# A Mamba-2 scan and a low-rank mixer on one core: a new order for the first third of a hand-kept instruction list, and a last tile in two halves

## The chip, the cores and the metric

One of the eight cores of a Trainium2 chip. The metric is device time in microseconds for one execution, the median of several runs. Engines: PE (TensorE, matmuls; PEld is its weight load), DVE (VectorE), ACT (ScalarE), POOL (GpSimd), SP (SyncE, which issues DMAs here).

## The reference

```
# scan: x (4,8,768,32), a (4,8,768), B and C (4,8,768,16)
cum = cumsum(log(clip(a)))                    # in chunks of 32 positions
M   = (C B^T) * exp(cum_i - cum_j) * causal   # within a chunk
y   = M x + (C state) * exp(cum)
state = exp(sum) * state + sum_j B_j x_j exp(cum_last - cum_j)
# bridge: y -> x2 (4, 768, 256): batch, position, channel
# mixer: U (768,32), V (32,768), w_ch1 (256,1024), w_ch2 (1024,256)
u   = x2 + ((x2^T U) V)^T
out = u + relu(u w_ch1) w_ch2
```

The scan's inputs and the output are float32. U, V, w_ch1 and w_ch2 arrive as 64-bit floats, and the kernel first makes them into 32-bit numbers from their words.

## The kernel before

**Tiling.** The scan works on twelve pairs of blocks of 128 positions (three pairs for each of four batches; eight heads together). The mixer of a batch works on two halves of 384 positions and eight blocks of 128 of the 1024 hidden columns.

**Order.** Nothing is scheduled by a tool: PLAN (line 34) is a list of words, and follow (line 915) goes through it and issues each word's instructions. Every engine runs its own in that order, so a word's place decides what stands behind what on each queue. The words, with pair k, batch b, half j, hidden block m:

- Loads, all issued on SP: Bk (two loads of B, one of C), Xk (two loads of x), U, V (four loads), w0 to w8 (pieces of the two weights). A leading Y marks the early ones. B, X and w without Y are held (line 920, `until`) until the last DVE instruction issued before that word is done, and SP stands still meanwhile.
- c1 to c9: one step each of making a weight piece into 32 bits (to_fp32, line 409): first two DVE word steps and one ACT step, then one DVE word step, then one POOL addition; c0 converts U, C0 converts V. v spreads V over the partitions (spread, line 872): an ACT rounding into Vn, a DVE subtraction in UV (line 875), sixteen small matmuls (line 880), four ACT copies.
- A0, A1: the decays (line 369). K: the factors between chunks.
- Scan of a pair: P or Q (multiply B and C by decays, DVE, line 466), T or V (transposes on PE, then ACT and DVE copies T and Cm), g (sixteen matmuls, line 522), m and M (DVE masks, four in all), s (sixteen matmuls, line 556), u (DVE updates of S, then Sm on POOL, line 583), i and j (line 646, j waiting for a small DVE copy into `settled` or for another DVE instruction of that turn), n (32 matmuls, line 681), y (two ACT copies out of PSUM, line 693), t or O (transposes back, line 701).
- Mixer of batch 0: p, q (lines 728 and 746), a (line 756 and a DVE addition to yT), U b.j.m (first weight, plain float32, two matmuls over 384 positions, line 800), d (second weight, output, line 831). Batches 1 to 3 use f, e, h in place of U, with weights split by R and activations split by S.
- Fn: the next PSUM tile that is asked for is first written by n blocks of a 128-column product with the identity (fill and idle, lines 132 and 156). A second F ahead of the next tile replaces the first.

The words tiles hold the 64-bit words; there are 15 of them. PSUM has eight tiles, two for each of the tags w, x, z and y.

**The last tile.** d3.1.0.5 is the list's last word. When an output tile (128 positions, 256 channels) has its last product, lines 854 to 856 add it on DVE to ytok and store it from SP.

Of the kernel before, what the change touches and what calls it, by code (L numbers as in the profile page):

```python
# [23 lines left out]
ALU = mybir.AluOpType  # L24
# [7 lines left out]


PLAN = (
    'F3 YU0 c0 A0 YB0 Q0.1 Q0.0 A1 F2 Q0.2 V0.0.0 YX0 YB1 V0.1.1 c0 Q1.0 YX1 F1 K0 s0 g0 Q1.2 m0 '
    'V1.0.2 YB2 Q1.1 V1.1.2 M0 n0 YX2 u0 g1 i0 s1 Q2.0 M1 YV0 j0 y0 m1 Q2.2 Q2.1 V2.0.2 F1 u1 '
    'V2.1.3 C0 C0 n1 C0 YB3 w1 i1 g2 j1 y1 w0 m2 B5 s2 F3 X3 c0 M2 v0 B4 O0.0 u2 t1 i2 n2 j2 P3 T3 '
    'c1 y2 T3 O2.1 c2 p0 P5 g3 w4 T5 m3 M3 q0 c1 c1 w2 c2 T5 n3 a0.1 X4 a0.0 s3 U0.1.0 c2 U0.1.1 B6 '
    'P4 T4 u3 w3 w6 T4 U0.0.1 c5 c5 i3 c3 c5 g4 j3 y3 s4 w5 m4 U0.0.0 U0.1.6 c3 U0.1.7 M4 c3 X5 u4 '
    'U0.0.6 B8 c4 U0.0.3 P6 t3 c4 T6 T6 i4 R0 g5 R3 n4 s5 c7 M5 U0.0.7 c4 U0.1.5 U0.0.4 w8 j4 y4 w7 '  # L40
    'X6 c7 c7 m5 B9 U0.1.3 c6 U0.0.2 c6 c6 U0.1.4 u5 n5 i5 B7 g6 c9 j5 y5 M6 c9 t4 c9 U0.0.5 U0.1.2 '
    'd0.0.1.0 m6 c8 c8 B10 R1 t5 d0.0.2.0 R5 d0.0.2.1 p1 c8 d0.0.2.2 X7 q1 R6 d0.0.1.1 P7 d0.0.1.2 '
    'R0 T7 R2 R1 T7 a1.0 d0.0.2.3 d0.0.1.3 a1.1 d0.1.0.0 S1.0 P10 d0.1.0.1 d0.1.0.2 d0.1.0.3 s6 R3 '
    'R2 X8 g7 n6 m7 X9 P9 M7 X11 f1.0.0 u6 f1.0.4 f1.0.1 e1.0.0 h1.0.0 f1.0.5 e1.0.4 h1.0.4 e1.0.1 '
    'f1.0.6 i6 s7 d0.0.0.0 R5 R4 f1.0.7 h1.0.1 R4 d0.0.0.1 P8 u7 T8 T8 e1.0.6 h1.0.6 e1.0.7 '
    'd0.0.0.2 d0.0.0.3 h1.0.7 e1.0.5 f1.0.2 h1.0.5 j6 f1.0.3 d0.1.2.0 e1.0.2 y6 e1.0.3 R6 d0.1.1.0 '
    'h1.0.2 X10 S1.1 d0.1.1.1 T9 T9 d0.1.1.2 h1.0.3 d0.1.1.3 d0.1.2.1 d0.1.2.2 d0.1.2.3 s8 n7 i7 u8 '
    'g8 R7 j7 m8 M8 s9 R7 f1.1.0 R7 R4 R5 d1.0.0.0 d1.0.0.1 d1.0.0.2 d1.0.0.3 u9 e1.1.0 d1.0.1.0 '
    'f1.1.7 d1.0.1.1 d1.0.1.2 h1.1.0 y7 f1.1.6 R6 e1.1.7 d1.0.0.4 d1.0.0.5 t7 d1.0.1.3 e1.1.6 '
    'h1.1.6 d1.0.2.0 d1.0.2.1 d1.0.2.2 h1.1.7 f1.1.4 d1.0.2.3 d1.0.1.4 d1.0.1.5 f1.1.1 d1.0.2.4 B11 '  # L50
    'e1.1.4 h1.1.4 e1.1.1 d1.0.2.5 h1.1.1 t6 f1.1.3 f1.1.2 f1.1.5 e1.1.3 e1.1.2 h1.1.2 i8 n8 s10 j8 '
    'e1.1.5 d1.1.0.0 d1.1.2.0 d1.1.2.1 d1.1.1.0 P11 d1.1.1.1 u10 h1.1.3 d1.1.1.2 d1.1.0.1 d1.1.2.2 '
    'd1.1.0.2 h1.1.5 d1.1.0.3 d1.1.1.3 y8 d1.1.2.3 d1.1.0.4 d1.1.1.4 d1.1.0.5 d1.1.2.4 d1.1.2.5 '
    'd1.1.1.5 t8 i9 g9 m9 T10 T10 M9 p2 n9 q2 g10 m10 M10 T11 T11 j9 a2.0 s11 g11 u11 y9 m11 i10 '
    'S2.0 M11 n10 t9 f2.0.0 f2.0.4 e2.0.0 f2.0.1 h2.0.0 f2.0.5 e2.0.1 h2.0.1 f2.0.2 j10 e2.0.4 y10 '
    'e2.0.5 e2.0.2 f2.0.3 h2.0.4 i11 n11 h2.0.5 h2.0.2 e2.0.3 f2.0.6 f2.0.7 h2.0.3 j11 y11 a2.1 '
    'e2.0.7 e2.0.6 h2.0.6 d2.0.0.0 S2.1 h2.0.7 t10 t11 d2.0.0.1 d2.0.0.2 f2.1.1 f2.1.0 d2.0.0.3 '
    'e2.1.1 e2.1.0 h2.1.0 h2.1.1 f2.1.3 d2.0.0.4 d2.0.0.5 f2.1.2 p3 d2.0.2.0 d2.0.1.0 d2.0.2.1 '
    'e2.1.2 h2.1.2 d2.0.1.1 q3 d2.0.2.2 e2.1.3 d2.0.2.3 f2.1.4 d2.0.1.2 d2.0.1.3 d2.0.2.4 f2.1.5 '
    'h2.1.3 e2.1.4 h2.1.4 d2.0.2.5 e2.1.5 h2.1.5 d2.0.1.4 d2.0.1.5 f2.1.6 f2.1.7 a3.0 e2.1.6 '  # L60
    'd2.1.0.0 e2.1.7 h2.1.6 a3.1 d2.1.2.0 d2.1.2.1 d2.1.0.1 d2.1.0.2 S3.0 f3.0.2 h2.1.7 f3.0.0 '
    'd2.1.0.3 f3.0.1 d2.1.0.4 e3.0.2 h3.0.2 d2.1.0.5 e3.0.0 h3.0.0 e3.0.1 f3.0.3 d2.1.1.0 d2.1.2.2 '
    'd2.1.1.1 d2.1.1.2 d2.1.1.3 e3.0.3 f3.0.6 d2.1.2.3 h3.0.3 h3.0.1 f3.0.4 f3.0.7 e3.0.6 f3.0.5 '
# [10 lines left out]
def kernel(  # L74
# [27 lines left out]
    nc = tc.nc  # L102
    P = 128
    NB, NH, S, D = x.shape
    N = B.shape[-1]
    NC = S // P
# [33 lines left out]
    def bank(tag, *dims):  # L140

        t = psum.tile([P, 4 * P], FP32, tag=tag, name=tag, bufs=BANKS[tag])
        if fills[0]:
            idle(t, fills[0])
        fills[0] = 0
        n = 1
        for d in dims:
            n *= d
        t = t[:, :n]
        if len(dims) == 1:  # L150
            return t
        names = "abcd"[:len(dims)]
        return t.rearrange(f"p ({' '.join(names)}) -> p {' '.join(names)}",
                           **dict(zip(names[1:], dims[1:])))
# [8 lines left out]
    class Kept:  # L163
# [6 lines left out]
        def __getattr__(self, name):  # L170
# [8 lines left out]
    vector = Kept(nc.vector)  # L179
# [7 lines left out]
        out=a_sb,  # L187
        in_=a.rearrange("(g b) h (c s) -> g (b h c) s", g=2, s=P).rearrange(
            "g r s -> r g s"))
# [44 lines left out]
    w1 = [const.tile([P, NCB, DF], FP32R, name=f"w1{i}") for i in range(3)]  # L234
    w1all = mix.tile([P, NQ, NCB, W], FP32, tag="u", name="w1f", bufs=1)
    w1f = [w1all[:, c] for c in range(NQ)]
    w2 = [const.tile([P, NM, DM], FP32R, name=f"w2{i}") for i in range(2)]
# [23 lines left out]
    U2, V2, w12, w22 = (w.bitcast(INT32) for w in (moe_U, moe_V, moe_w_ch1, moe_w_ch2))  # L261
# [58 lines left out]
    for v in range(2):  # L320
        half = slice(v * H, v * H + H)
        vector.tensor_tensor(out=ref[half, half], in0=upto[half, half],
                                in1=low[v][half, half], op=ALU.subtract)
# [18 lines left out]
    for g in range(2):  # L342
# [3 lines left out]
        out=la.rearrange("p b c h -> p b h c"),  # L346
        in0=la_ps.rearrange("p g (b h c) -> p (g b) h c", h=NH, c=NC),
# [108 lines left out]
    behind = {"turn": 0, "first": []}  # L456
# [261 lines left out]
    def mixer(b):  # L718
# [63 lines left out]
        def products(t, pairs, start):  # L782
            for lhsT, rhs in pairs:
                nc.tensor.matmul(out=t, lhsT=lhsT, rhs=rhs, start=start, stop=True,  # L784
                                 skip_group_check=True)
                start = False

        def scaled(t):
            nc.scalar.activation(t, t, AF.Copy, scale=1.0 + EPS)  # L789
# [41 lines left out]
        def down(j, k, n):  # L831

            parts = b or j >= PLAIN
            pieces = 6 if parts else 4

            def weight(v, m):
                return w2[v][:, m] if v < 2 else w2b[m // 2][:, m % 2]

            if n == 0:
                gs["o", j, k] = bank(TAGS.get((b, j), "xzx")[k], DM)  # L840
            t = gs["o", j, k]
            c = HS // P * j + k
            if parts:
                v, half = divmod(n, 2)
                products(t, [(gs[j, m // 2][v][:, m % 2, ts(k, P)], weight(v, m))
                             for m in range(NQ * half, NQ * half + NQ)], n == 0)
                if n == 3:
                    scaled(t)
            else:
                products(t, [(gT[j, n][:, m, ts(k, P)], w2f[n][:, m]) for m in range(2)], n == 0)  # L850
            if n == pieces - 1:
                products(t, [(Vs[:, ts(c, P)], ps)], False)
                o = ytok[b][:, c]
                behind.setdefault(
                    "part", vector.tensor_tensor(out=o, in0=t, in1=o, op=ALU.add))
                nc.sync.dma_start(out=out[b, ts(c, P)], in_=o)

        us, gs, gT = {}, {}, {}
        return SimpleNamespace(p=project, q=parted, a=added, S=split, f=first, e=second, h=third,
                               d=down, U=plain)  # L860


# [24 lines left out]
    yT[0] = mix.tile([P, NCB, S], FP32, tag="yT", name="yT")  # L887
    ytok[0] = mix.tile([P, NC, DM], FP32, tag="ytok", name="ytok")
    mx = {0: mixer(0)}


# [23 lines left out]
    def follow(plan):  # L915

        for word in plan.split():
            name, rest = (word[:2], word[2:]) if word[0] in "YZ" else (word[0], word[1:])
            at = [int(v) for v in rest.split(".")]
            if name in "BXw":  # L920
                until[:] = [vector.last]
            if name[0] in "YZ":
                issuer[0] = nc.scalar if name[0] == "Z" else nc.sync
                early[name[1]](*at)
                issuer[0] = nc.sync
            elif name in loads:
                loads[name](*at)
            elif name in scans:
                scans[name](*at)
            elif name in whole:  # L930
                whole[name](*at)
            else:
                b, *at = at
                if b not in mx:
                    mx[b] = mixer(b)
                getattr(mx[b], name)(*at)
            until.clear()
# [32 lines left out]
```

## Time and profile before

| what | value |
|---|---|
| median of 3 runs | 224.45 us (224.22 to 224.62) |
| profiled execution, whole | 225.48 us |
| its span | 223.8 us |
| granted PE clock | 1.00 in every stretch |
| last product ends, last sum ends | 220.53, 220.99 us |
| DMA busy share, 5 to 15 us | 0.94 and 0.92 |

The profile is one execution. Its span runs from the first to the last instruction; the whole time has 1.7 us more around it. Busy time of PE is modelled at its ends, so two short idle stretches can hide in it.

| load | issued at, us | landed after, us |
|---|---|---|
| U | 1.25 | 3.1 |
| pair 0: B, C, B | 1.74, 2.32, 2.94 | 3.2, 3.3, 3.2 |
| pair 1: x | 8.18, 8.80 | 3.0, 3.3 |
| pair 2: B, C, B | 9.74, 10.39, 11.21 | 2.9, 3.1, 4.6 |
| pair 2: x | 12.05, 12.68 | 4.0, 4.2 |
| V, four loads | 14.96 to 16.50 | 2.3, 2.2, 2.8, 3.3 |

SP has some 25 loads to issue in the first 22 us, each 0.4 to 0.8 us when nothing holds it.

### The profile page before, as it was taken

What the parts mean: (1) busy time and instruction counts of PE and PEld (TensorE: products, weight loads), DVE (VectorE), ACT (ScalarE), POOL (GpSimd) and SP (SyncE); (2) the same over time, 40 slices, a digit from 0 to 9 for tenths busy, and PEclk for the clock granted to TensorE, in tenths of its full rate; (3) what the DMA queues carried; (4) which work ended last, traced back from release to release, by engine and by line L of the source; (5) the groups of instructions that cost most, each with busy time, mean ns of one, the idle gap of its engine ahead of it and who ended that gap; (6) DMA issues with size and microseconds to landing.
All of it is one profiled execution on the core that took longest, in us unless ns stands there. A gap on an engine that the chain in (4) does not pass through costs nothing.

```text
span 223.8 us, 7019 instructions
## 1 busy us (share of the span) xinstructions
PE 215.5 (96%) x3016; PEld 182.8 (82%) x3016; DVE 144.5 (65%) x313; ACT 108.6 (49%) x251; POOL 31.8 (14%) x44
## 2 busy tenths in 40 slices
PE   7878999999999999999999999999999999999994
PEld 4655665675667898888999996888989999999993
DVE  4686499758245876767665925968945954586631
ACT  3335655484657347571436123577535455554510
POOL 3013011522367024203100100000000000000000
PEclk9999999999999999999999999999999999999999
DMA  6985799898824154004005001000000100100011
GB/s 100 134 114 86 137 157 209 217 175 237 100 35 59 50 96 73 28 0 92 8 23 94 6 24 51 3 3 3 0 26 1 47 0 26 46 1 28 23 47 47
DMA packets 69519, 14.57 MB, mean 65 GB/s; under 512 B 63792, under 2 KB 67696, under 8 KB 69488
## 3 DMA queue, kind: packets, MB, share of 16 engines
q1 hardware_dynamic: 69488, 14.13, 32.0%
q8 instruction: 23, 0.38, 0.8%
q14 instruction: 8, 0.07, 0.1%
HBM read 10.98 MB, written 3.15 MB: 63 GB/s over the span
## 4 chain that ended last, share of the span: by engine, by line
PE 89%; SPq 7%; DMA 1%; DVE 1%; issue 1%; ACT 0%; DVEq 0%
PE x L784 31%; PE z L784 24%; PE y L784 12%; SPq L202 6%; PE y L681 4%; PE y L646 4%; PE w L482 2%; PE w L701 2%; PE x L522 2%; PE w L556 2%; DMA words<-in_moe_V_dram 1%; PE z L522 1%; PE w L728 1%; PE w L746 1%; PE x L756 1%; PE z L756 1%
## 5 line engine op out<-in xcount | busy, mean ns | idle before, releaser
L784 PE MATMUL x<-u,w 128*128 128x384 f32 x144 | 33.4, 344 | 0.0
L784 PE MATMUL z<-u,w 128*128 128x384 f32 x144 | 33.0, 343 | 0.0
L174 DVE SCALAR_TENSOR_TENSOR words<-words 128x768 fp32r<-128x768 f32 (+3 forms) x35 | 29.8, 855 | 1.9 <-DVE words L174 0.5
L789 ACT ACTIVATE x<-x 128x384 f32<-128x384 f32 (+1 forms) x30 | 13.6, 455 | 28.1 <-PE x L784 28.1
L174 DVE SCALAR_TENSOR_TENSOR words<-x,words 128x384 fp32r<-128x384 f32 x24 | 13.3, 556 | 18.7 <-ACT words L819 16.2
L784 PEld LDWEIGHTS z<-u,w 128*128 128x128 f32 x144 | 24.5, 188 | 0.7 <-ACT z L789 0.2
L784 PEld LDWEIGHTS x<-u,w 128*128 128x128 f32 x144 | 24.2, 188 | 0.8 <-ACT x L789 0.2
L784 PE MATMUL x<-w2c,words 128*128 128x256 f32 x112 | 22.6, 339 | 0.0
L784 PEld LDWEIGHTS x<-w2c,words 128*128 128x128 f32 x112 | 18.3, 189 | 1.7 <-POOL words L443 0.4
L789 ACT ACTIVATE z<-z 128x384 f32<-128x384 f32 (+1 forms) x27 | 12.6, 465 | 14.7 <-PE z L784 14.4
L784 PE MATMUL y<-w,words 128*128 128x256 f32 x144 | 19.6, 283 | 0.0
L784 PEld LDWEIGHTS y<-w,words 128*128 128x128 f32 x144 | 18.8, 190 | 0.1
L583 POOL TENSOR_TENSOR Sm<-S,own 128x256 f32<-128x256 f32 (+1 forms) x12 | 7.0, 582 | 68.0 <-DVE S L174 44.3
L174 DVE SCALAR_TENSOR_TENSOR words<-z,words 128x384 fp32r<-128x384 f32 x24 | 13.2, 551 | 4.8 <-ACT words L819 4.8
L819 ACT ACTIVATE words<-x 128x384 fp32r<-128x384 f32 x24 | 11.8, 492 | 6.4 <-PE x L784 6.4
L819 ACT ACTIVATE words<-z 128x384 fp32r<-128x384 f32 x24 | 11.9, 494 | 6.1 <-PE z L784 6.1
L784 PE MATMUL x<-w,words 128*128 128x256 f32 x96 | 13.9, 286 | 0.0
L784 PEld LDWEIGHTS x<-w,words 128*128 128x128 f32 x96 | 12.7, 190 | 0.4 <-DVE ytok L174 0.3
L646 PEld LDWEIGHTS y<-T,Sm 32*64 32x64 f32 x352 | 8.8, 131 | 5.2 <-issue 2.3
L646 PE MATMUL y<-T,Sm 32*64 32x64 f32 x352 | 12.3, 239 | 0.6 <-DVE settled L174 0.5
L174 DVE SCALAR_TENSOR_TENSOR S<-S,kept,w 128x64 f32<-128x64 f32 x40 | 11.2, 280 | 1.6
L522 PE MATMUL x<-Cm,T 32*64 32x128 f32 x192 | 11.3, 306 | 1.0 <-issue 0.6
(151 smaller groups left out, 401.3 us busy)
## 6 DMA issues: line engine op xcount, KB each, us to landing
words<-in_moe_w_ch_dram SPq DMA_DIRECT2D x7, 512.0 KB, 5.1
x<-in_x_dram SPq DMA_DIRECT2D x24, 128.0 KB, 3.9
out_dram<-ytok SPq DMA_DIRECT2D x24, 128.0 KB, 1.7
bc<-in_B_dram SPq DMA_DIRECT2D x24, 64.0 KB, 3.3
bc<-in_C_dram SPq DMA_DIRECT2D x12, 128.0 KB, 3.2
words<-in_moe_w_ch_dram SPq DMA_DIRECT2D x2, 256.0 KB, 3.8
words<-in_moe_U_dram SPq DMA_DIRECT2D x1, 192.0 KB, 3.1
words<-in_moe_V_dram SPq DMA_DIRECT2D x4, 48.0 KB, 2.8
```

The lines of the kernel that those rows point to most:

```text
L174: self.last = call(*args, **kwargs)
L202: op = issuer[0].dma_start(**kwargs)
L482: nc.tensor.transpose(out=tp[:, i, v], in_=s["BC"][:, i, c + v].rearrange("p h n -> p (h n)"), identity=ident)
L522: nc.tensor.matmul(out=s["g"][r][cols, c], lhsT=s["T"][rows, 0, c, cols], rhs=s["Cm"][rows, :, :, ts(2 * c + p, Q)].rearrange("r v t i -> ...
L556: nc.tensor.matmul(out=s["A"][p][ts(r, Q), v], lhsT=s["BC"][half, 0, v, 2 * r:2 * r + 2].rearrange("p h n -> p (h n)"), rhs=x_sb[k][half, ...
L583: nc.gpsimd.tensor_tensor(out=s["Sm"][:, sl], in0=s["S"][:, sl].rearrange("p i (s d) -> p i s d", s=2), in1=own2[:, b, 4 * q + sl.start:4 ...
L646: product = nc.tensor.matmul(out=channels(k)[p][ts(v, H), c, n], lhsT=own[ts(r, Q)], rhs=st[k]["T"][ts(r, Q), 1, :, ts(2 * c + p, Q)].rear ...
L681: behind["first"].append(nc.tensor.matmul(out=y[p][ts(i, Q), c, n], lhsT=x_sb[k][half, c, h], rhs=s["M"][half, h // 2, c, h % 2], start=fr ...
L701: nc.tensor.transpose(out=t[:, c, g], in_=yT[b][:, g, ts(2 * q + c, P)], identity=ident)
L784: nc.tensor.matmul(out=t, lhsT=lhsT, rhs=rhs, start=start, stop=True, skip_group_check=True)
L789: nc.scalar.activation(t, t, AF.Copy, scale=1.0 + EPS)
L819: nc.scalar.activation(gs[j, m // 2][0][:, m % 2], t, AF.Relu, scale=NEAR)
```

## The change

The list up to the word `a1.1` has a new order; from there on both lists have the same words in the same order. In the new order

- SP issues B0, X0, B1, B2, then U, X1, V, X2, B5, B3, w0, w1, X3, B4, w2, w4 and so on; before it was U, B0, X0, B1, X1, B2, X2, V, B3, w0, w1, B5, X3, B4, w4, w2;
- U's conversion stands behind pair 1's first masks, not ahead of the decays;
- Q2's transposes stand behind n1, and a fill of four blocks (F4) ahead of n1;
- u2 stands ahead of pair 2's masks and of UV, O0.0 and T3 behind j2;
- a0.0, the weights' loads and conversions, the sixteen U words and the first d words have other places; U0.1.7 comes last of the U words, right ahead of a1.1;
- there are 12 fill blocks in all, before 10. The first fill is of two blocks, before three.

The sum and store of the last output tile of the last batch become two: each half of 128 channels is added and stored by itself, the first from SP, the second from ACT.

```diff
 PLAN = (
-    'F3 YU0 c0 A0 YB0 Q0.1 Q0.0 A1 F2 Q0.2 V0.0.0 YX0 YB1 V0.1.1 c0 Q1.0 YX1 F1 K0 s0 g0 Q1.2 m0 '
-    'V1.0.2 YB2 Q1.1 V1.1.2 M0 n0 YX2 u0 g1 i0 s1 Q2.0 M1 YV0 j0 y0 m1 Q2.2 Q2.1 V2.0.2 F1 u1 '
-    'V2.1.3 C0 C0 n1 C0 YB3 w1 i1 g2 j1 y1 w0 m2 B5 s2 F3 X3 c0 M2 v0 B4 O0.0 u2 t1 i2 n2 j2 P3 T3 '
-    'c1 y2 T3 O2.1 c2 p0 P5 g3 w4 T5 m3 M3 q0 c1 c1 w2 c2 T5 n3 a0.1 X4 a0.0 s3 U0.1.0 c2 U0.1.1 B6 '
-    'P4 T4 u3 w3 w6 T4 U0.0.1 c5 c5 i3 c3 c5 g4 j3 y3 s4 w5 m4 U0.0.0 U0.1.6 c3 U0.1.7 M4 c3 X5 u4 '
-    'U0.0.6 B8 c4 U0.0.3 P6 t3 c4 T6 T6 i4 R0 g5 R3 n4 s5 c7 M5 U0.0.7 c4 U0.1.5 U0.0.4 w8 j4 y4 w7 '
-    'X6 c7 c7 m5 B9 U0.1.3 c6 U0.0.2 c6 c6 U0.1.4 u5 n5 i5 B7 g6 c9 j5 y5 M6 c9 t4 c9 U0.0.5 U0.1.2 '
-    'd0.0.1.0 m6 c8 c8 B10 R1 t5 d0.0.2.0 R5 d0.0.2.1 p1 c8 d0.0.2.2 X7 q1 R6 d0.0.1.1 P7 d0.0.1.2 '
-    'R0 T7 R2 R1 T7 a1.0 d0.0.2.3 d0.0.1.3 a1.1 d0.1.0.0 S1.0 P10 d0.1.0.1 d0.1.0.2 d0.1.0.3 s6 R3 '
+    'YB0 F2 A0 Q0.1 Q0.0 YX0 A1 F2 Q0.2 V0.0.0 V0.1.1 YB1 Q1.0 K0 F1 s0 YB2 YU0 Q1.1 YX1 g0 Q1.2 m0 '
+    'YV0 V1.0.2 Q2.0 M0 V1.1.2 n0 g1 u0 i0 Q2.1 s1 j0 y0 m1 YX2 c0 F4 M1 n1 B5 C0 Q2.2 V2.0.2 YB3 '
+    'u1 V2.1.3 w0 c0 C0 C0 i1 w1 s2 g2 u2 m2 c0 j1 F5 F3 y1 M2 v0 X3 t1 i2 B4 n2 j2 w2 y2 P3 O0.0 '
+    'T3 T3 w4 c1 c2 O2.1 P5 c1 c1 p0 g3 m3 M3 X4 q0 P4 T5 T5 n3 w7 c2 a0.1 c2 R0 s3 u3 a0.0 B6 '
+    'U0.1.0 T4 T4 c3 U0.1.1 U0.0.1 i3 c5 g4 c5 c5 j3 s4 y3 U0.0.0 w3 U0.1.6 m4 u4 U0.0.6 w5 t3 c3 '
+    'c3 U0.0.3 U0.1.2 M4 P6 X5 T6 T6 c4 i4 c6 g5 n4 B7 c4 c6 c4 c8 s5 w6 j4 m5 M5 y4 U0.0.2 U0.0.5 '
+    'n5 u5 i5 g6 c8 c8 j5 y5 t4 M6 m6 c7 c7 c7 U0.1.5 w8 t5 U0.1.4 U0.0.7 c9 U0.0.4 p1 c6 d0.0.1.0 '
+    'd0.0.1.1 c9 R0 R1 R3 q1 d0.0.1.2 X7 U0.1.3 X6 P7 R1 d0.0.2.0 d0.0.2.1 R5 T7 T7 R2 B8 B10 '
+    'd0.0.2.2 a1.0 c9 R6 B9 d0.0.2.3 d0.0.1.3 U0.1.7 a1.1 d0.1.0.0 S1.0 P10 d0.1.0.1 d0.1.0.2 '
+    'd0.1.0.3 s6 R3 R2 X8 g7 n6 m7 X9 P9 M7 X11 f1.0.0 u6 f1.0.4 f1.0.1 e1.0.0 h1.0.0 f1.0.5 e1.0.4 '
...
                 o = ytok[b][:, c]
-                behind.setdefault(
-                    "part", vector.tensor_tensor(out=o, in0=t, in1=o, op=ALU.add))
-                nc.sync.dma_start(out=out[b, ts(c, P)], in_=o)
-
-        us, gs, gT = {}, {}, {}
+                stored.append(c)
+                if b < NB - 1 or len(stored) < NC:
+                    behind.setdefault(
+                        "part", vector.tensor_tensor(out=o, in0=t, in1=o, op=ALU.add))
+                    nc.sync.dma_start(out=out[b, ts(c, P)], in_=o)
+                else:
+                    for queue, cols in ((nc.sync, ts(0, P)), (nc.scalar, ts(1, P))):
+                        vector.tensor_tensor(out=o[:, cols], in0=t[:, cols], in1=o[:, cols],
+                                             op=ALU.add)
+                        queue.dma_start(out=out[b, ts(c, P), cols], in_=o[:, cols])
+
+        us, gs, gT, stored = {}, {}, {}, []
```

## The prediction

> **What bounds the kernel now.** I read the page's first parts, then a table of busy time by stretch, then the timeline of each engine up to 53 us, with lines 174, 202, 784 and 856 followed back to the words of the list. The page first:
>
> ```profile
> span 223.8 us, 7019 instructions
> PE 215.5 (96%) x3016; PEld 182.8 (82%) x3016; DVE 144.5 (65%) x313; ACT 108.6 (49%) x251; POOL 31.8 (14%) x44
> ...
> q8 instruction: 23, 0.38, 0.8%
> ```
>
> The stretches (length, then busy us of PE, PEld, DVE, ACT, POOL, then granted clock and DMA share) say where PE's missing 8.3 us lie:
>
> ```profile
> 0.00:5.00 5.00, 3.57 (x8) 1.98 (x9) 2.61 (x13) 1.91 (x3) 2.06 (x12) 1.00 0.57 100
> 5.00:10.00 5.00, 4.89 (x68) 3.55 (x73) 2.80 (x11) 1.96 (x6) 0.00 (x0) 1.00 0.94 123
> 10.00:15.00 5.00, 3.88 (x157) 2.57 (x152) 4.15 (x14) 1.93 (x7) 0.95 (x2) 1.00 0.92 126
> 15.00:20.00 5.00, 3.55 (x146) 2.74 (x143) 3.07 (x13) 1.89 (x7) 0.62 (x1) 1.00 0.39 75
> 20.00:25.00 5.00, 4.59 (x152) 2.93 (x144) 3.23 (x12) 2.75 (x10) 1.66 (x3) 1.00 0.87 165
> 25.00:30.00 5.00, 4.61 (x132) 2.67 (x110) 2.96 (x9) 3.55 (x9) 0.00 (x0) 1.00 0.75 106
> 30.00:75.00 45.00, 44.96 (x619) 30.86 (x620) 29.82 (x70) 27.18 (x58) 17.75 (x16) 1.00 0.72 145
> ```
>
> From 30 us to the last product PE has no room: the time is PE's work plus what it stands idle before 30 us (4.9 us) plus the 3.3 us behind its last product. So an order of the first third can win at most those 4.9 us, and every idle stretch it opens later goes to the end whole. The timeline names the waits that the new order touches (start, length, engine, line, what, and in brackets the idle time before it):
>
> ```profile
> 5.05 0.85 PE L377 MATMUL w<-la,ref 128*128 128x192 f32 x2
> 15.90 0.41 PE L556 MATMUL w<-x,BC 64*32 64x64 f32 x19 [0.83 <-issue]
> 19.95 0.43 DVE L174 TENSOR_SCALAR words<-words 128x192 f32<-128x192 f32 x2 [1.76 <-DMA words<-in_moe_V_dram]
> 22.37 0.36 DVE L174 TENSOR_TENSOR UV<-UV,Vn 128x192 f32<-128x192 f32 x1 [0.21 <-ACT Vn L874]
> 32.73 0.56 DVE L174 TENSOR_TENSOR yT<-x,yT 128x384 f32<-128x384 f32 x1
> 33.44 1.54 PE L784 MATMUL x<-yT,w1f 128*128 128x384 f32 x4
> 220.57 0.42 DVE L174 TENSOR_TENSOR ytok<-y,ytok 128x256 f32<-128x256 f32 x1 [0.64 <-PE y L784]
> ```
>
> To see there: V's words stop DVE for 1.76 us; the first U product (33.44) starts right behind DVE's first addition to yT (32.73 to 33.29).
>
> **The change, part by part.** Times are those of the profiled execution, the new order's worked out from its rows.
>
> *A, up to j0 (before: ends 16.73).* The fill ahead of the first decay product is two blocks, not three: three took from 3.77 to 5.05, so 0.43 each; la was ready at 4.44. The decays come 0.43 earlier. DVE is then without a gap from 8.24 to 13.5; it loses U's last word step (0.35) and gains a BC piece (0.28), and waits for pair 1's second B, now in SP's ninth place (6.23 to 6.9, landing some 3.1 later, so about 9.7). Of the 0.43 I keep 0.15: S ends 13.35, Sm 14.1, i0 14.15. s1 needs pair 1's x, which moves behind pair 2's B, C and U: SP's places 14 and 15 (10.39 and 11.21 in the old queue), so it lands at 13.5 and 14.4 to 15.4 instead of 11.2 and 12.1. That costs nothing while PE waits in the middle of s1 anyway: the 0.83 us ended at 15.90, with no tile named. The trace's 16 KB packets of the instruction queue ran from 12.96 to 14.44 and from 17.14 to 18.63, and PE stood 0.83 and 0.62 us some 1.3 us behind each; the second stop came 127 matmul records after the first. The instruction count up to s1 is the same, so I let the stop end at 15.75. Without that cover PE waits for x itself, to 15.4, which is still sooner; only if x shares the fate of the old queue's load of 11.21 (landed at 15.81, across a code packet) is s1 0.1 later. Sum at j0: -0.15 (bounds -0.43 and +0.1).
>
> [...]
>
> *B, from j0 to the end of v0 (before: 16.73 to 23.37, 6.64 us).* Before, Q2's four transposes ran while ACT copied y0. Now n1 comes first, behind a fill of four blocks (F4) which waits for the first y0 copy (0.38) and takes 0.86 (0.215 a block, as the 384-column fill's 0.64 at 21.86 gives): j0 ends 16.58, fill 17.0 to 17.9, n1 (0.86) to 18.75, transposes (0.6) to 19.35. DVE cannot start Cm before that, and its order is now Cm 0.61, two word steps 0.72, three S 0.91, four M 1.5, UV 0.36, where before M and UV came ahead of S: 4.1 us plus small gaps, UV done at 23.5. v0's second group of four products waits for it (before 22.73), and the rest takes 0.45: v0 ends 23.9, +0.53 to before, so B costs 0.68. The other arm hides below that: V must land, then words 0.43, BC 0.41, S 1.30, Sm 0.62, then i1, s2, g2 (1.6) and M. With V at 17.15 or earlier this arm is no later than the first. V's four loads sit in places 16 to 19 (12.05 to about 13.6); the old ones there landed at 16.05 and 16.88, V itself took 2.2 to 3.3, and SP's issue at 12.68 was held 2.23 us while code was loaded. So V lands between 16.2 and 17.7; I take 17.0, and the late end costs 0.55 more. The 1.76 us stall is thus mostly gone, but what was behind it is not earlier. On ACT, U's and V's word steps now stand ahead of the copies of Q2's transposes: done at 17.4, 1.7 before those are asked for. On SP, B5 is now held by pair 1's last M (16.6), with B3, w0, w1 and X3 behind it; B5's old neighbours left at 16.97 to 25.67, so none of these is later than it was.
>
> *C, to the end of g3 (before 29.97).* Same PE work; t0's transposes move from ahead of i2 into the 0.14 us wait for BC ahead of T3. -0.14, g3 ends at 30.36.
>
> *D, g3 to the first U product (before 3.47 us).* DVE: M 1.42, ps 0.43, then now BC 0.69 and one word step 0.42 instead of two word steps 0.76, then the addition 0.56, with gaps 3.8. PE's own work there is the 3.47 of before, a0.0 included. +0.33.
>
> *E, the U products.* New weight order w2, w4, w7, w3, w5, w6, w8. All words of w2 and w4 come some 3 us sooner. w5's load is held by DVE's last S of pair 4 (about 42); a 512 KB load lands 5.1 later, 47.2; DVE then has 1.2 (two steps), 0.73 twice, 1.2 and the tiny copy that j4 waits for: 51.2. PE adds up to j4 at 50.75. With 0.15 of the same kind at j3: +0.35 taken, bounds 0 and 0.7. w3, w6 and w8 by the same sums land 2 us or more ahead of their products; their cover gone, each costs its lateness whole.
>
> *F, the last tile.* One sum of 0.42 becomes two. 128-column sums of this kind (BC) took 0.49 for two, so the second half is ready 0.07 later. The store of 128 KB took 1.7 from issue to landing; a half on ACT's queue, unused so far, is not in the trace. Bounds: half the time (-0.85), or the same with SP's longest store issue, 1.00 for 0.33 (+0.67). I take the same, since 48 KB of V took 2.2 and 96 KB of a 2.1. +0.07.
>
> [...]
>
> Sum: -0.15 + 0.68 - 0.14 + 0.33 + 0.35 + 0.07 = +1.14 on the span of 223.8, so 224.9. That execution took 225.48 in all (1.7 around its span), 1.0 over the median of 224.45; I put the difference on the median: 225.5 after rounding down, as the small gaps I added may be hidden.
>
> **The rivals.**
>
> *Faster.* V's stall goes, and the DVE queue of B and D does not bind, because DVE starts its steps earlier than I let it (V landed by 16.2, Cm not behind the transposes of 19.35). Then A gives -0.43, B the 0.62 and 0.30 idle ahead of 20.89 less 0.43 for two more fill blocks, C -0.14: about -1.0, some 223.5 (223.2 to 224.0). For it: 4.9 us are idle there. Against: n1 behind F4 and the Q2 transposes behind n1 are in PE's own order. It decides if UV is done by 22.7.
>
> *No change.* A's full 0.43 and C against B's 0.68, E and D hidden: 224.4.
>
> *V late.* The code load holds SP within V's loads: V at 17.7, +0.55: 226.1. For it the 2.23 us issue at 12.68; against it V's short issues (0.42).
>
> *A weight late.* w8 (held by w6's last word step) or w3 comes over 1 us behind its product: 227. Against: 2 us to spare by E's sums.
>
> *Code in time.* s1 does not stop for code and waits for x alone: it resumes at 15.4, not 15.75, and B's queue with it: 0.35 less, 225.1. Against: both code packets before 20 us were followed by a stop. [...]
>
> **How the numbers follow.** Forecast 40%, V late 14%, weight late 5%, code in time 4%, faster 24%, no change 13%. A measurement of this kernel tells about 0.2% (0.45 us) from no change, so faster 0.24, same 0.13, slower 0.63. The likeliest case alone spans 224.8 to 226.3 (E and F at their nearer bounds); the range reaches down into the faster case and up past V late: 223.6 to 226.6.
>
> **What would show it.** Right: L377 at about 4.6; DVE's stall at V below 0.7; F4's fill at 17.0 and n1 at 17.9; UV's subtraction ending past 23.3; the first U product idle before it, at 34.0 or later, released by yT's addition; the last store landing within 0.2 of before, relative to the last product. Wrong: first U product by 33.3, or PE idle below 4.5 us in all before it; a wait of over 1 us between 35 and 75 us that ends on a weight's load.

## The result, and the profile after

The changed kernel takes 226.34 us (median of 4 runs, 225.44 to 226.62), the kernel before 224.48 (4 runs, 224.22 to 224.62): 1.0075 times as long, 95% interval 1.0046 to 1.0103. Two later comparisons gave 1.0152 (1.0113 to 1.0191) and 1.0140 (1.0092 to 1.0188). The sign is sure; the size was not the same each time, and whether that is the chip is not shown.

The profiled execution is the fastest of its four (225.44, span 223.7), while the one of before was 1.0 above its median. So the two profiles differ by nothing in the whole and are good for the places only. The page of after:

```profile
span 223.7 us, 7023 instructions
PE 216.2 (97%) x3016; PEld 183.5 (82%) x3016; DVE 145.3 (65%) x313; ACT 108.8 (49%) x251; POOL 32.2 (14%) x44
...
q8 instruction: 23, 0.38, 0.6%
...
q10 hardware_dynamic: 144, 0.07, 0.1%
```

TensorE has as many products as before: the two more fill blocks make fills wider, not more. DVE has one sum more and one small copy less, and q10 is ACT's new store. Busy time by stretch of the same execution (length; PE, PEld, DVE, ACT, POOL; granted clock, DMA share, GB/s):

```profile
5.00:10.00 5.00, 5.00 (x80) 3.81 (x86) 2.78 (x9) 1.97 (x6) 0.00 (x0) 1.00 1.04 134
10.00:15.00 5.00, 4.00 (x176) 2.60 (x162) 3.64 (x15) 1.93 (x7) 0.99 (x2) 1.00 0.74 135
15.00:20.00 5.00, 4.07 (x130) 2.55 (x134) 4.26 (x17) 2.46 (x8) 0.99 (x2) 1.00 0.84 117
20.00:25.00 5.00, 4.50 (x164) 2.93 (x158) 2.43 (x8) 2.37 (x8) 1.29 (x3) 1.00 0.80 157
25.00:30.00 5.00, 4.75 (x101) 3.04 (x83) 3.69 (x11) 3.30 (x9) 0.69 (x1) 1.00 0.84 121
```

PE stands about 4.1 us in the first 30, before 4.9. The timeline of its DVE (start, length, engine, line, what, and in brackets the idle time before it and what ended that; "issue" is idle time that the profile lays to nothing):

```profile
15.33 0.42 DVE L174 TENSOR_SCALAR words<-words 128x192 f32<-128x192 f32 x2
...
16.33 0.42 DVE L174 TENSOR_SCALAR words<-words 128x192 f32<-128x192 f32 x2
...
20.04 0.91 DVE L174 SCALAR_TENSOR_TENSOR S<-S,kept,w 128x64 f32<-128x64 f32 x3 [0.55 <-issue]
...
22.20 0.35 DVE L174 TENSOR_TENSOR UV<-UV,Vn 128x192 f32<-128x192 f32 x1
...
32.67 0.56 DVE L174 TENSOR_TENSOR yT<-x,yT 128x384 f32<-128x384 f32 x1
```

The first line is U's word steps, the second V's. V's have no bracket: the 1.76 us stall is gone, V had landed. UV is done at 22.55 (before 22.73), the first U product starts at 33.38 (before 33.44). Up to there the new order costs nothing against the profile of before. But that one was slow for its kernel: a second profile of the same kernel (`before_again` below, span 223.0) has its first U product at 32.69 and UV done at 21.99. Against it even this fastest execution is 0.7 us late, and the other executions lose more.

### The profile page after: what moved, and what is told of

Its sections match the earlier page's. It is cut to its first block, busy times and chain, and to the rows that moved or that the text cites. A ratio compares the mean times of both kernels' runs of the same rounds, so it can differ in the third digit from the quotient of the medians.

```text
span 223.7 us, 7023 instructions
## 1 busy us (share of the span) xinstructions
PE 216.2 (97%) x3016; PEld 183.5 (82%) x3016; DVE 145.3 (65%) x313; ACT 108.8 (49%) x251; POOL 32.2 (14%) x44
## 4 chain that ended last, share of the span: by engine, by line
PE 93%; issue 2%; DVE 1%; POOL 1%; ACT 1%; DVEq 0%; POOLq 0%
PE x L784 31%; PE z L784 24%; PE y L784 12%; PE y L646 4%; PE y L681 4%; PE w L482 2%; PE w L701 2%; PE x L522 2%; PE w L556 2%; PE z L522 1%; PE w L728 1%; PE w L746 1%; PE x L756 1%; PE x L136 1%; PE w L136 1%
## 5 line engine op out<-in xcount | busy, mean ns | idle before, releaser
L789 ACT ACTIVATE x<-x 128x384 f32<-128x384 f32 (+1 forms) x30 | 13.6, 455 | 27.0 <-PE x L784 26.8
L583 POOL TENSOR_TENSOR Sm<-S,own 128x256 f32<-128x256 f32 (+1 forms) x12 | 7.6, 631 | 69.1 <-DVE S L174 46.1
L646 PE MATMUL y<-T,Sm 32*64 32x64 f32 x352 | 13.0, 239 | 0.8 <-POOL Sm L583 0.5
L646 PEld LDWEIGHTS y<-T,Sm 32*64 32x64 f32 x352 | 9.3, 131 | 4.9 <-issue 2.0
L174 DVE TENSOR_TENSOR BC<-bc,F 128x512 f32<-128x512 f32 (+2 forms) x18 | 10.7, 605 | 1.6 <-ACT F L384 1.6
```

The costliest lines, as they stand in the source:

```text
L174: self.last = call(*args, **kwargs)
L583: nc.gpsimd.tensor_tensor(out=s["Sm"][:, sl], in0=s["S"][:, sl].rearrange("p i (s d) -> p i s d", s=2), in1=own2[:, b, 4 * q + sl.start:4 ...
L646: product = nc.tensor.matmul(out=channels(k)[p][ts(v, H), c, n], lhsT=own[ts(r, Q)], rhs=st[k]["T"][ts(r, Q), 1, :, ts(2 * c + p, Q)].rear ...
```

## Experiments

Theories at the start. T1: the new list lengthens the queues behind DVE, some 1.1 us inside the span (the prediction's). T2: the loss is outside the span, through the second store queue. All ratios below are to the kernel before, run in turn on the same chip (median 224.95 to 225.11 there); three chips were used, so kernels may differ by chip as well.

### The parts apart

`before_again` and `after_again` are the two kernels unchanged. `list_only` has the new PLAN with the old tail, `tail_only` the old PLAN with the new tail:

```diff
# tail_only: PLAN of before, and
+                    for queue, cols in ((nc.sync, ts(0, P)), (nc.scalar, ts(1, P))):
+                        vector.tensor_tensor(out=o[:, cols], in0=t[:, cols], in1=o[:, cols],
...
```

> The kernel before against itself. All theories: a ratio of 1.000 within 0.002. What it is for: how far one program's executions lie apart, and whether the profiled execution before (span 223.8, 225.48 in all) is a typical one. If the median of 224.5 is right for it, most executions have a span near 222.8.

> The changed kernel once more. All theories: again about 1.0075 (226.2 us). Theory 1 (the new list's queues behind DVE cost about 1.1 us inside the span): its span lies some 1 us above that of the kernel before in the same job. Theory 2 (the cost lies outside the span, with the second store queue): spans within 0.3 us of each other, and the time around the span some 1 us longer.

> The new list with the old last tile. Theory 1: +1.07 on the kernel before, 225.5, nearly all of the change. Theory 2: within 0.5 us of the kernel before, 224.5 to 224.9.

> The old list with the last tile in two halves. Theory 1: +0.07, a ratio of 1.000 to 1.001. Theory 2: +1.0 to +1.8, ratio 1.005 to 1.008, with the last product no later in the span than before.

| kernel | ratio, 95% | runs whose mean clock is 0.992 or below |
|---|---|---|
| before_again | 0.9996 (0.9967 to 1.0025) | 5 of 12 |
| tail_only | 1.0005 (0.9977 to 1.0034) | 7 of 12 |
| list_only | 1.0106 (1.0069 to 1.0143) | 8 of 10 |
| after_again | 1.0152 (1.0113 to 1.0191) | 6 of 6 |

T2 falls: the tail alone is worth nothing that its interval (0.5 us faster to 0.8 slower) can show. The loss is the list's: 1.0106 is 2.4 us, over twice what T1 says. (after_again lies above list_only by 0.5%, with intervals that overlap.) The last column was in no theory. after_again's profiled execution (span 227.1) has it in place; busy time by stretch:

```profile
15.00:20.00 5.00, 3.26 (x84) 1.74 (x76) 3.20 (x14) 2.20 (x7) 0.10 (x1) 1.00 0.73 110
20.00:25.00 5.00, 3.98 (x88) 2.70 (x88) 3.53 (x12) 1.27 (x4) 2.17 (x4) 0.58 0.93 171
25.00:30.00 5.00, 4.75 (x139) 3.22 (x139) 1.34 (x6) 2.11 (x7) 0.00 (x0) 0.74 0.81 113
```

The granted clock is 0.58 and 0.74: the clock's record says half speed from 20.79 to 27.61 us. And ahead of it, in the timeline of DVE, then of PE (in brackets: idle before it, and what ended that):

```profile
17.84 0.43 DVE L174 TENSOR_SCALAR words<-words 128x192 f32<-128x192 f32 x2 [1.62 <-DMA words<-in_moe_V_dram]
18.19 0.42 DVE L174 TENSOR_TENSOR BC<-bc,F 128x256 f32<-128x256 f32 x1
18.52 1.29 DVE L174 SCALAR_TENSOR_TENSOR S<-S,kept,w 128x64 f32<-128x64 f32 x4
```

```profile
18.66 0.55 PE L482 MATMUL x<-ident,BC 128*128 128x128 f32 x3 [0.74 <-DVE BC L174]
...
20.56 0.58 PE L646 MATMUL y<-T,Sm 32*64 32x64 f32 x14 [1.08 <-POOL Sm L583]
...
22.57 0.67 PE L646 MATMUL y<-T,Sm 32*64 32x64 f32 x16
23.70 1.65 PE L136 MATMUL y<-ident 128*128 128x384 f32 x2 [0.46 <-ACT yT L693]
```

Read it downwards. DVE stands 1.62 us at V's load and goes on at 17.84 (the last of V's four loads landed at 17.65; in after's profile at 15.82). Behind it in DVE's queue are Q2.2's product BC and u1's S, so PE waits 0.74 us for BC and 1.08 for Sm, which is made from S. Then the clock halves, and the last fill takes 1.65 us where after's takes 0.91: from j0 to the end of v0 it is 10.95 us, in after's profile 7.86. The kernel before stood 1.76 us at V too, but there V's conversion stood behind u1 and V2.1.3 in the list.

So three theories went on. L: a late V is the loss. Q: the length of DVE's queue ahead of UV, whatever V does (the prediction's step B). G: the clock closes because the new order leaves TensorE too little to do, whatever V does.

### V's conversion behind u1; more fills; thin fills

```diff
# v_later
-M1 n1 B5 C0 Q2.2 V2.0.2 YB3 u1 V2.1.3 w0
+M1 n1 B5 Q2.2 V2.0.2 YB3 u1 C0 V2.1.3 w0
# warm (C0 where the change has it; ... stands for words left out here)
-YV0 V1.0.2 ... n0 g1 ... C0 C0 i1
+YV0 F2 V1.0.2 ... n0 F1 g1 ... C0 C0 F2 i1
# thin_before: the kernel before, fills but the first on 32 rows and 32 columns (r = 32)
-lhsT=ident, rhs=ident[:, None, :] ...
+lhsT=ident[:r, :r], rhs=ident[:r, None, :] ...
```

> The changed kernel once more, as the measure for the other kernels on this chip. So far it stood at 1.0075 and 1.0152 times the kernel before. In its quick profile V's load had landed when DVE came to it, and the granted clock stayed at 1.00 from 7.6 to 222.7 us; in its slow one (span 227.1) DVE stood 1.62 us at V's load and the clock was at 0.5 from 20.79 to 27.61 us. Theory L (a late V is the loss): between 1.007 and 1.016, and in the profile DVE stands over 1 us at V's load wherever the span is over 225. Theory Q (the longer DVE queue ahead of UV is the loss, as the prediction had it): 1.005 with the span at 224 to 225, whatever V does.

> The changed kernel with one word moved: V's first conversion (two DVE steps and one ACT step that wait for V's load) stands behind u1's DVE updates, not ahead of Q2.2's. Theory L: Q2.2 and u1 no longer wait for V, PE gets its work at 17 to 20 us, the clock stays open, and the time falls to 0.999 to 1.004 times the kernel before, at least 1.0 us below the changed kernel of this job where that stands at 1.007 or more. Theory Q: the same DVE instructions stand ahead of UV, so no more than 0.3 us comes back. Theory G (the clock closes because the new order gives TensorE too little to do in some 3.41 us stretch, whatever V does): the clock of most runs stays at 0.992 or below and less than half of the loss comes back.

> The changed kernel with V's conversion left where it is and five more fill blocks of 128 columns (some 0.28 us of TensorE each): two ahead of the transposes of pair 1's C, one ahead of g1, two ahead of i1, each at a place where TensorE stood 0.33 to 1.1 us in the traces so far. If the closed clock makes up most of the loss (theories L and G share this), the runs' clock rises to 0.992 or more and the time falls 0.8 to 1.5 us below the changed kernel, though TensorE does 1.4 us more. If the stall at V itself costs the time and the clock little: within 0.4 us of the changed kernel. Theory Q: 0 to 0.6 us slower than it.

> The kernel before with its fills, but for the first, on a quarter of the rows and a quarter of the columns of the array: as many instructions, as long, a sixteenth of the multiplications. By the traces the clock closed behind 3.41 us windows in which rows times columns times time came to 0.26 of a full array or less (0.26 and 0.17), and stayed open at 0.27; the busy share of those windows was 0.73 and 0.46, while windows of 0.67 and 0.70 busy in the kernel before stayed open. If the gate counts the array's share: more runs at 0.992 or below (15 of 39 runs of the kernel before were), the clock closes between 12 and 22 us, and the time is 0.3 to 1.5 us above the kernel before. If it counts busy time: clock and time as before, within 0.3 us.

| kernel | ratio, 95% | clock 0.992 or below |
|---|---|---|
| after_third | 1.0140 (1.0092 to 1.0188) | 6 of 6 |
| v_later | 1.0056 (1.0021 to 1.0091) | 5 of 10 |
| warm | 1.0176 (1.0127 to 1.0224) | 5 of 6 |
| thin_before | 1.0010 (0.9980 to 1.0039) | 6 of 12 |

One word moved gives back 226.67 against 228.58 us: 1.9 of the 3.5 us. So V's place in DVE's queue is more than half of the loss, as L says (a little less than it promised), and Q as the sole cause falls, since the same DVE instructions still stand ahead of UV. But L also had the clock stay open, and it closed in half of v_later's runs. Nor do the two kept profiles show the gain (spans 225.6 for after_third, 226.0 for v_later: one of the faster runs of the one, one of the slower of the other). First the fill F4 in list_only's profile and its DVE at V, then v_later's DVE at V (in after_third's it stood 1.69 us):

```profile
15.20 1.98 PE L136 MATMUL y<-ident 128*128 128x512 f32 x2 [0.47 <-ACT yT L693]
...
17.10 0.43 DVE L174 TENSOR_SCALAR words<-words 128x192 f32<-128x192 f32 x2 [1.38 <-DMA words<-in_moe_V_dram]
...
18.37 0.43 DVE L174 TENSOR_SCALAR words<-words 128x192 f32<-128x192 f32 x2 [0.74 <-DMA words<-in_moe_V_dram]
```

In list_only, after_third and v_later the clock went to half at 15.33, 16.14 and 16.20 us, at most 0.11 us after DVE came to V. There a late V did not close it. F4 and n1 at half speed lost 1.2 us in each, which is what after_third's stretch from j0 to the end of v0 has over after's (9.03 against 7.86); V's stall adds little to that there. Only in after_again (half speed from 20.79 us) and warm does the closed clock come behind a late V (1.62 and 2.54 us of stall) and idle products. Which of the two costs a typical run how much is not separated.

`warm` was a poor experiment: 0.9 us above after_third, the wrong way, though the intervals overlap. Its fills lay behind the waits that they were to lie in: a fill writes the tile that the next word asks for, and so begins only when that tile is free (PE still stood 0.54 us, and only then came the fill of 10.39 us). V's stall was 2.54 us in its profile, and the clock closed behind it all the same.

`thin_before` is inconclusive: no difference that its interval could show, and as many runs with a closed clock as the kernel before had (11 of 21 beside it).

What closes the clock can be read across the profiles in part. The clock's records fall on a grid of 3.41 us: after's record of the full clock, 7.62 to 222.66 us, is 63 times that long, v_later's of half the clock, 16.20 to 19.61, once. For each such window I summed, over its products, streamed columns times the rows and columns of the array used, and divided by the same sum in a stretch of U products. Eight of the nine windows behind which the clock went to 0.5 have 0.17 to 0.30; the ninth, in uv_later_fill (below), has 0.32, with PE busy 0.38 of it behind late weights. The clock stayed open behind windows down to 0.27, and behind every one above 0.32. Busy time draws no clean line either: PE was busy 0.38 to 0.74 of the closing windows, and 0.67 to 0.73 of some that did not close it. Scan products use 32 rows and 64 columns or the like, so a stretch of them looks busy and counts little; but that this is what the clock goes by is a reading, and thin_before, its one test, does not bear it out. The kernel before lives at the same edge: 43 of its 105 runs on these chips, its own copy included, had 0.992 or below (one window at half speed is 1.7 us in 225), at little cost (medians of spans 0.1 to 0.7 us apart).

The grid lies differently against the kernel from one execution to the next: the first record of the full clock begins at 4.84 to 7.87 us in these profiles (6.85 in before's, 7.62 in after's). And no closing window was idle, as the 0.38 to 0.74 above say.

### U later, the fill sooner, the weights' conversions later

v_later's profile showed what was left: half speed from 16.20 to 19.61 us, F4 of 2.08 us in it instead of 1.13, n1 of 1.18 instead of 0.86. F4 came just after the poor window.

```diff
# uv_later = v_later and U's three steps behind M2, n2, T3
-w0 c0 C0 C0 i1 w1 s2 g2 u2 m2 c0 j1 ... M2 v0 X3 ... n2 j2 ... w4 c1
+w0 C0 C0 i1 w1 s2 g2 u2 m2 j1 ... M2 v0 c0 X3 ... n2 c0 j2 ... w4 c0 c1
-YX2 c0 F4
+YX2 F4
# v_later_fill = v_later and the four blocks in a tile of their own
-F4 M1 n1
+E4 M1 n1        # E: idle(bank("x", 4 * P), n)
# uv_later_fill = both
# loads_last = v_later_fill and
-w4 c1 c2 O2.1 P5 c1 c1 p0 g3 m3 ... q0 P4 T5 T5 n3 w7 c2 a0.1 c2 R0
+w4 O2.1 P5 p0 c1 c2 g3 c1 c1 m3 ... q0 T5 T5 n3 w7 a0.1 P4 c2 c2 R0
```

> The changed kernel with V's first conversion behind u1, as in v_later (1.0056 times the kernel before), and with U's three conversion steps moved from between pair 1's masks and pair 2's masks to places behind M2, n2 and T3. DVE has 0.73 us less ahead of UV (0.42 us for the two word steps, 0.31 for the third). Theory Q (the length of DVE's queue ahead of UV sets v0): 0.5 to 0.7 us below v_later, 1.002 to 1.003. If the clock sets the rest (theory G: v_later's profiled run had it at 0.5 from 16.20 to 19.61 us, F4 took 2.07 us and not 1.12): within 0.3 us of v_later, with half of the runs at 0.992 or below.

> The changed kernel with V's first conversion behind u1, and with the four fill blocks F4 written into a PSUM tile of tag x of their own, not into the tile that n1 writes next. F4 waited 0.47 us for ACT's copies out of that tile and lay behind the 3.41 us stretch in which TensorE does least; the blocks now begin as soon as pair 1's first masks have been read, about 0.5 us earlier. Theory G: more of the runs than v_later's 5 of 10 at 0.997 or above, and the time 0.5 to 1.3 us below v_later (1.000 to 1.003 times the kernel before). If the clock is no part of it: at most the 0.47 us of the wait. Theory Q: within 0.2 us of v_later, since UV stands at the end of DVE's queue whatever TensorE does.

> Both edits in one. If queue and clock each have a share: the lowest of the three and 0.998 to 1.001 times the kernel before. If only one counts: as the better of the two.

> v_later_fill (1.0047 times the kernel before; its open clock bought nothing) with the conversions of the first two weight pieces moved behind O2.1, P5 and p0, so that the copies to ytok no longer stand on DVE behind a load, and with P4's multiplication and one step of c2 moved behind a0.1. In v_later_fill's profile DVE stood 0.9 us at two loads of the first weight between 25 and 26.5 us (2.8 us in uv_later_fill's), TensorE 0.32 us for ytok behind it (2.2 us), and 0.69 us ahead of the first U product for yT, behind BC (0.69) and a word step (0.42). Theory L, widened (each load that DVE stands at hands its lateness on, and what was won ahead of it is lost there): no wait of DVE on a weight ahead of ytok, the first U product 0.7 to 1.2 us earlier than 33.42 us, the time 0.7 to 2.0 us below v_later_fill, 0.996 to 1.002 times the kernel before. If the loss sits behind the first U product (code, later weights): within 0.4 us of v_later_fill. Theory G alone: as v_later_fill, since it leaves the clock as it is.

| kernel | ratio, 95% | clock 0.992 or below |
|---|---|---|
| uv_later | 1.0044 (1.0011 to 1.0077) | 6 of 12 |
| v_later_fill | 1.0047 (1.0011 to 1.0082) | 2 of 12 |
| uv_later_fill | 1.0046 (1.0018 to 1.0074) | 4 of 12 |
| loads_last | 1.0050 (1.0024 to 1.0076) | 2 of 12 |

Four kernels, one time. The three with the sooner fill had a closed clock in 8 of 36 runs, the two with V's word moved and the fill as it was (v_later, uv_later) in 11 of 22. That is the way G says, though on different chips; to the time it did nothing that can be measured. U's steps out of DVE's queue, which Q priced at 0.5 to 0.7 us, gave 0.1% with intervals that overlap. v_later_fill's profile shows one way in which such a gain goes. By the end of v0 it was 1.0 us ahead of after (22.20 against 23.19; how much of that is a clock that opened at 4.84 and not 7.62 is not shown), and then its DVE and PE read:

```profile
25.50 0.50 DVE L174 TENSOR_SCALAR words<-words 128x256 f32<-128x256 f32 x2 [0.41 <-DMA words<-in_moe_w_ch_dram]
26.47 0.50 DVE L174 TENSOR_SCALAR words<-words 128x256 f32<-128x256 f32 x2 [0.47 <-DMA words<-in_moe_w_ch_dram]
26.88 0.75 DVE L174 COPY ytok<-z 128x256 f32<-128x256 f32 x2
...
31.66 0.69 DVE L174 TENSOR_TENSOR BC<-bc,F 128x512 f32<-128x512 f32 x1 [0.69 <-issue]
...
32.27 0.42 DVE L174 SCALAR_TENSOR_TENSOR words<-words 128x256 int32<-128x256 int32 x1
...
32.72 0.56 DVE L174 TENSOR_TENSOR yT<-x,yT 128x384 f32<-128x384 f32 x1
...
33.42 1.53 PE L784 MATMUL x<-yT,w1f 128*128 128x384 f32 x4 [0.69 <-DVE yT L174]
```

DVE stands at the next load (the first weight, 0.41 and 0.47 us), and the copies to ytok wait behind it. By the end of g3 0.4 us of the lead are gone. Then BC (itself 0.69 us late, by nothing the profile names) and a word step stand ahead of yT's addition, and the first U product starts at 33.42: after's 33.38, the whole lead spent. loads_last takes these steps out of the way. In its profile no DVE instruction waits for a weight ahead of ytok and none stands between M and yT but the ps step, as meant; but the time did not move. The profile can't say why: that execution had the clock closed from 21.52 to 24.94, so its first U product came at 34.47. PE also stood 0.58 us at 36.5 for S, which P4's BC and a word step now precede:

```profile
34.50 0.68 DVE L174 TENSOR_TENSOR BC<-bc,F 128x512 f32<-128x512 f32 x1
35.10 0.42 DVE L174 SCALAR_TENSOR_TENSOR words<-words 128x256 int32<-128x256 int32 x1
...
36.50 0.63 PE L482 MATMUL w<-ident,BC 128*128 128x128 f32 x4 [0.58 <-DVE S L174]
```

So theory L in its widened form falls: with DVE's waits for weights taken out of the way the kernel was no faster. What stays open is the last 0.45% (1.0 us): in runs with an open clock the repaired lists have spans of 223.9 to 224.2 (medians), the kernel before 222.9 to 223.15. Single profiles show pieces of it, all behind the reordered stretch: PE stood 0.49 us (after_third) and 0.69 us (v_later) in the middle of g5 at 56 us with no tile named, some 1 us behind the end of a packet of the instruction queue (54.96 and 55.19; 53.16 in after's, where PE came there 1.3 us behind it and did not stop). And in the last 13.5 us ahead of the last product's end the new list takes 0.2 us longer than the old one, though the words there are the same; uv_later and uv_later_fill, which differ from it in the first third alone, do not. Whether the places of the instruction queue's packets have a part in that was not tried. No version here beats the kernel before.

## Why the prediction was right in time and wrong in its reasons

The time of 225.5 (223.6 to 226.6) held the 226.34, and "slower" was right. Its steps, by after's profile (before's time, then after's):

| step | forecast | after's profile | what the runs add |
|---|---|---|---|
| A, up to j0 | -0.15 | -1.40 (16.73, 15.33) | 14.73 to 16.04 in the ten profiles of new lists, 16.23 to 17.19 in the four of the old: holds |
| B, j0 to the end of v0 | +0.68 | +1.22 (6.64, 7.86) | 10.95 in after_again: V late, clock closed |
| C, to the end of g3 | -0.14 | -0.15 (6.60, 6.45) | |
| D, to the first U product | +0.33 | +0.27 (3.47, 3.74) | the 0.69 us of v_later_fill |
| E, to the first f1 product | +0.35 | -0.32 (46.36, 46.04) | wrong; no product waited for a weight |
| to the last product | 0 | +0.30 (140.73, 141.03) | 0.2 of it in the last 13.5 us; open, above |
| F, tail | +0.07 | +0.04 (3.24, 3.28) | tail_only 1.0005 |

*A* was mis-sized because of one assumption, that s1 would stop until 15.75 as before. In all four profiles of the old list PE stands 0.81 to 0.97 us in the middle of s1 with no tile named, and the first code packet had ended 0.03 to 0.30 us ahead of s1's start. In the ten profiles of new lists it ends 1.9 to 2.5 us ahead (in after's at 12.45, s1 starting at 14.46), and none stops there with no tile named; six wait for x instead. So the rival "Code in time", given 4%, describes A. That the packet is what PE stood for in the old list rests on these times alone.

*B* has the failed step. It let the other arm, which begins at V, "hide below", with V at 17.0 and "the late end costs 0.55 more". In after's profile V came in time and the clock was open, and B was still 0.5 over its sum: 0.2 ahead of n1's end (F4 took 1.05 to n1's start, for 0.86), 0.1 on DVE, 0.2 behind UV (0.64 to the end of v0, as in the profile of before, where 0.4 was reckoned). Even there the other arm did not hide: u2's S waits 0.55 us (20.04) and starts right behind s2, which stands behind V's words, BC, u1's S and Sm. In after_again's V landed at 17.65, about the 17.7 set as the latest, and B took 3.1 us more than in after's, no 0.55: DVE stood 1.62 us, all that PE could have done meanwhile was behind that in DVE's queue (PE was busy 3.26 us of the 5 from 15 to 20), and from 20.79 us the clock was at half. So the rival "V late" (14%, 226.1) is the one that the median agrees with, and v_later shows its weight in later runs: moving V's conversion alone gave 0.84% back. For the result's own four runs it is not shown: only the fastest was profiled, and just one had a mean clock below 0.992. The clock was in no step and no rival; the profile of before, at 1.00 throughout, gave no sign of it.

*D* had the right number for another reason, by luck: the forecast was that yT's addition on DVE holds the first U product, but in after's profile that addition ends at 33.23, PE is idle for 0.03 us ahead of the product, and 0.24 of the 0.27 us are PE's own busy time in the stretch. The wait forecast does come where PE is earlier (0.69 us in v_later_fill). *E* was wrong in sign in after's profile, and in reason in all: over the ten profiles of new lists it ran from -0.57 to +0.45, the three largest with the stops at g5 (after_third, v_later) and loads_last's wait for S, and no product waited for a weight. *F* was right: its +0.07 lies within tail_only's interval (0.5 us faster to 0.8 slower), and the 0.85 us that half of the store's 1.7 us would give lies outside it.

Of its marks, L377 at 4.52, the store (landing 2.20 us behind the last product, before 2.17) and a stall at V below 0.7 fit after's profile; the stall does not fit after_again's or after_third's. F4's fill at 15.81 (forecast 17.0), n1 at 16.86 (17.9), UV done at 22.55 (past 23.3) and the first U product (34.0) do not; and PE idle below 4.5 us before that product, its mark for wrong, came true (4.1). Sum and result agree because A's gain was underrated and the price of a late V and of the clock left out, and the two errors nearly cancel. The agreement is luck, and only in part: 1.05 us was forecast over the median before, 1.86 measured.

## What to carry to other kernels

An instruction that waits for a load belongs behind everything on its engine that TensorE needs within the load's spread of arrival, even if the load had landed in the one profile at hand: moving one word behind u1 was worth 1.9 us of 3.5. Judge an order by several executions and by each one's clock and span; the profile here was the fastest of four, and the one of before was slow for its kernel. Look for the 3.41 us window in which TensorE does least, by the array's area as well as by busy time: here the clock closed behind windows of up to 0.32 by the one and 0.74 by the other, and the kernel before, which has windows at 0.27, had a closed clock in 43 of 105 runs.

## What the runs showed of the hardware that was not expected

- The clock went to half behind windows of 3.41 us in which PE was busy 38 to 74% of the time, where its products came to 0.17 to 0.32 of what a stretch of U products does.
- With the clock at half the fill F4 took 1.98 us (list_only) and 2.08 (v_later), at the full clock 1.13 (after). n1 behind it took 1.18 in both, at the full clock 0.86 (after). The clock had gone to half at 15.33 us in list_only, where F4 starts at 15.20, and at 16.20 in v_later.
- The same load of V (four times 48 KB) was complete between 15.8 and 18.4 us in executions of nearly the same list. Its last part was issued at 13.6 to 14.8 us in these ten; what differs more is the way from there. In 13 of all 14 profiles, the old list's among them, it took 3.0 to 3.8 us and landed 1.03 to 1.19 us behind the end of the second code packet. In after's it was issued at 13.93, took 1.89 us and landed at 15.82, ahead of that packet's end (16.37). So whether V was late went with the order of this load and that packet. No run moved the one without the other, so that the packet holds the load up is not shown.
